# A delta-rule attention and gated feed-forward kernel: joins unit by unit, the second pair's joins moved into the first pair's hops, far corrections behind a copy

## The chip, the cores and the metric

One core of one Trainium2 chip runs the kernel. The metric is the device time of one execution in microseconds (us). A profile gives, for one execution, a span (from the first to the last recorded instruction) and the start and length of each instruction. TensorE is called PE (its weight loads PEld), VectorE DVE, ScalarE ACT, GpSimd POOL, SyncE SP.

## The reference

Two parts follow each other. The first is a delta-rule recurrence over time for 4 batches and 8 heads, with sequences of 768 and heads of 48:

```
k_n = k / (norm(k) + 1e-6)
for t in range(768):
    y[t]  = q[t] @ state
    v_old = k_n[t] @ state
    state = state + beta[t] * outer(k_n[t], v[t] - v_old)
```

The second takes y as x, 3072 tokens by 384, through a feed-forward layer with w_in (384 by 2048) and w_out (2048 by 384):

```
h = x @ w_in
out = (h * sigmoid(1.702 * h)) @ w_out
```

The weights w_in and w_out arrive as 64-bit floats; the kernel turns them into 32-bit ones itself.

## The kernel before

**Units.** The sequence is cut into 6 chunks of 128 steps; a unit is one chunk of one batch, 24 in all. Units 0 to 3 (chunk 0 of the four batches) are of class `Step` and are worked on as two pairs, units 0 and 1, then 2 and 3. All later ones are of class `Half` and go through `slot`; the change leaves those alone.

**The solve of one unit.** Within a chunk the recurrence is a triangular system. It is cut into four blocks of 32 steps (`NB`, `BS`). The inverse of each 32 by 32 diagonal block is computed on DVE in halves of 16 (`invert`), and `merge` joins the halves of the first chunk: a product psP of 32 small matmuls per unit, a copy by ACT, a product psZ of 32 small matmuls and one of 128 by 128 per unit, a copy back by ACT. `merge` also transposes the inverses on DVE. Then a unit goes block by block: `solve` multiplies a block's right-hand side by the block's inverse (one 32 by 32 matmul for each of 8 heads, into psU), `solved` copies the result to SBUF on ACT, `below` multiplies it into the blocks underneath (into psV, for every head and every block below), and `rest` copies the next block's sum out of psV on ACT. Two units alternate: a hop is one call of `together`, which solves a block of one unit and does the `below` of the other. A pair takes 8 hops. The program's matmuls in 32-bit floats appear as two instructions each in the profile: 8 solves are 16 instructions.

**What stands around the hops.** Every engine runs its instructions in the order in which the program gives them (most go through `pinned`, which keeps program order). `fill(us)` puts pieces of the weight conversion into the program: DVE operations, and one ACT operation for each piece, called the clamp here (the Relu in `conversion`, with `low` as bias), that DVE waits for one piece later. `feed` puts three feed-forward products (ph) of the first tokens into the program. `warm(n)` puts in matmuls whose result is not used. `turn` transposes the keys of a later unit (psT), `gram` multiplies them (psG), `send_blocks` and `load_diagonals` bring the diagonal blocks through DRAM to the lanes of DVE (NT). `roots_second` scales the keys of units 4 to 7. `paced` lets POOL hold back a transfer of w_in until a hop is done; `fetch_out` starts a transfer of w_out. `put_out` makes the outputs (psY) and state of a unit, and ACT and small DMAs bring them to xT, which the ph products read.

**Order before.** Both joins of units 0 and 1, mixed with the scores of unit 3 and warm matmuls; 8 hops of the first pair (psU, psV), with four `turn`, two `gram` and warm matmuls between them; two `put_out`; both joins of units 2 and 3; then 8 hops of the second pair with a `feed` behind each; two `put_out`; a loop of 25 steps with `fill(1.0)` and `feed` each, in which DVE inverts the diagonal blocks of units 4 to 7 (`invert(1)`) and ACT scales keys; then the out products (po) of the first tokens, which start with 16 of one kind, and `slot` for the rest of the run.

Of the kernel before, what the change touches and what calls it, by code (L numbers as in the profile page):

```python
# [18 lines left out]
def kernel(  # L19
# [23 lines left out]
    C = 128  # L43
# [337 lines left out]
    def fill(us):  # L381
        while us > 0:
            us -= next(behind, us)
# [82 lines left out]
    def roots_second(areas):  # L466

        z, r = (TW[:, a : a + B * H].rearrange("p (b h) -> p b h", b=B) for a in (1792, 1856))
        for o in range(2):
            vec.tensor_reduce(z[:, 2 * o : 2 * o + 2], areas[o], axis=AX.X, op=ALU.add)  # L470
        pool.tensor_tensor(r, z, half[:, 0:1].broadcast_to([128, B, H]), op=ALU.pow)
        yield
        vec.tensor_scalar(r, r, 1e-6, None, op0=ALU.add)
        vec.reciprocal(r, r)
        for o in range(B):
            K = home(B + o)[:, :, 0:D]
            vec.tensor_tensor(K, K, r[:, o].broadcast_to([128, H, D]), op=ALU.mult)
            if o % HB == 1:
                yield
# [254 lines left out]
    def merge(pair, area, banks):  # L734

        XT, Pm = (
            [area[:, a + i * n : a + (i + 1) * n].rearrange("p (h k) -> p h k", h=H) for i in range(HB)]
            for a, n in ((0, H * BS), (HB * H * BS, H * BS // 2))
        )
        Z, HS = [inverse[X.n] for X in pair], BS // 2  # L740
        rows = [slice(k * BS, (k + 1) * BS) for k in range(NB)]
        for X, t in zip(Z, XT):
            vec.transpose(t.rearrange("p h k -> p (h k)"), X.rearrange("p h k -> p (h k)"))
        for X, x, m in zip(pair, Z, Pm):
            ps = banks[0][0].tile([128, H, HS], F32, tag=banks[0][1], name="psP")
            for h in range(H):
                for r in rows:
                    pe.matmul(
                        ps[r, h, :], lhsT=X.G[r, h, r], rhs=x[r, h, HS:], start=True, stop=True,
                        skip_group_check=True,  # L750
                    )
            act.activation(m, ps, ACT.Copy, scale=upper)
            yield
        for x, t, m in zip(Z, XT, Pm):
            ps = banks[1][0].tile([128, H, HS], F32, tag=banks[1][1], name="psZ")
            pe.matmul(ps, lhsT=ident, rhs=x[:, :, HS:], start=True, stop=True, skip_group_check=True)
            for h in range(H):
                for r in rows:
                    pe.matmul(
                        ps[r, h, :], lhsT=t[r, h, :], rhs=m[r, h, :], start=False, stop=True,  # L760
                        skip_group_check=True,
                    )
            act.copy(x[:, :, HS:], ps)
            yield

    def bank(name, shape=(128, H, D), big=False):
        if late:
            return one_bank(name)[:, 0 : H * D].rearrange("p (h d) -> p h d", h=H)
        from_, tag = (ps_big, "big") if big else (ps_seq, "seq")
        return from_.tile(list(shape), F32, tag=tag, name=name)  # L770
# [3 lines left out]
    class Step:  # L774
# [63 lines left out]
        def gather(self):  # L838
# [3 lines left out]
                start=True, stop=True, skip_group_check=True,  # L842
            )

        def below(self, blk, h, psR):
            r = slice(blk * BS, (blk + 1) * BS)
            for k in range(blk + 1, NB):
                u = slice(k * BS, (k + 1) * BS)
                pe.matmul(
                    self.psV[u, h, :], lhsT=self.G[r, h, u], rhs=self.U[r, h, :],  # L850
                    start=False, stop=True, skip_group_check=True,
                )

        def rest(self, blk, psR):
            u = slice((blk + 1) * BS, (blk + 2) * BS)
            act.copy(self.V[u], self.psV[u])

        def solve(self, blk, h, psU):
            r = slice(blk * BS, (blk + 1) * BS)
# [429 lines left out]
    def together(solves, belows):  # L1289

        solves = [(X, blk) for X, blk in solves if X]
        belows = [(X, blk) for X, blk in belows if X]
        psU = bank("psU") if solves else None
        psRs = [bank("psR") if X.n >= B else None for X, blk in belows]
        for h in range(H):
            for X, blk in solves:
                X.solve(blk, h, psU)
            for (X, blk), psR in zip(belows, psRs):
                X.below(blk, h, psR)
        for X, blk in solves:  # L1300
            X.solved(blk, psU)
        for (X, blk), psR in zip(belows, psRs):
            X.rest(blk, psR)
# [139 lines left out]
    for X in pair[:2]:  # L1443
        X.gather()
    warm(NY // 2)
    scaling = roots_second(areas)
    next(scaling)

    def paced(sign, i, j):

# [18 lines left out]
    products = merge(pair[:2], area, ((ps_seq, "seq"), (ps_big, "big")))  # L1469
    path, later = hops(*pair[:2]), hops(*pair[2:])  # L1470
    scored = pair[-1].scored
    for _ in range(HB):
        next(products)
        next(scored)
        warm(NM // 2)
    next(products)
    paced(inverse[0][0:1, 0, BS // 2 : BS // 2 + 1], 2, 1)
    fill(3.0)
    next(scaling)
    warm(NM)  # L1480
    Nds = []
    for i in range(2 * NB):
        together(*next(path))
        if i in (0, 1, 3, 5):
            at = pair[i % 2].US[i // 2 * BS : i // 2 * BS + 1, 0:1]
            paced(at, *{0: (2, 2), 1: (3, 0), 3: (3, 1), 5: (3, 2)}[i])
        if i == 0:
            warm(NM // 2)
            run(products)
            run(scored)  # L1490
            run(scaling)
        if i == 1:
            for X in pair[:2]:
                X.select()
        if i == 3:
            for b in range(HB, B):
                load_values(b, sync)
        if 1 <= i <= B:
            turn(B + i - 1)
        if i in (5, 6):  # L1500
            gram(B + i - 5)
        if i < 2 * NB - 1:
            warm(NU if i == 1 else NU // 2)
        if i == 6:
            Nds.append(send_blocks(B))
        if i > 5:
            fetch_out(i - 6, other_queue)
        fill(2.1 if i else 1.0)
    put_out(pair[0])
    merging = merge(pair[2:], area, ((ps_big, "big"), (ps_big, "big")))  # L1510
    fill(2.0)
    put_out(pair[1])
    Nds.append(send_blocks(B + 1))
    fetch_out(2, other_queue)
    for X in pair[2:]:
        next(merging)
        X.gather()
        warm(NM // 4)
    fill(4.0)
    for at in range(B):  # L1520
        for u in range(2):
            for half_ in range(2):
# [19 lines left out]
    ffn.append(hidden(xTs[0], gTs[0], slice(0, NTH), 1.3))  # L1542
    for i in range(2 * NB):
        if i == 0:
            for _ in range(HB):
                next(merging)
                fill(1.0)
            feed()
        together(*next(later))
        if i < 2:  # L1550
            gram(B + HB + i)
        if i == 1:
            Nds.append(send_blocks(B + HB))
        if i == 2:
            load_diagonals(Nds + [send_blocks(B + HB + 1)])
        feed()
        fill(2.2)
# [102 lines left out]
```

## Time and profile before

| | |
|---|---|
| time, median of 3 runs | 690.48 us (686.99 to 691.98) |
| the profiled execution | 683.09 us, its span 681.4 us |
| PE busy | 660.4 us (97%), 9290 matmul instructions |
| DVE busy | 479.5 us (70%) |
| ACT busy | 233.6 us (34%) |
| POOL busy | 269.4 us (40%) |
| granted clock of PE | 0.991 of full speed over the span |
| first solve of the first pair | 45.47 us |
| first solve of the second pair | 78.66 us |
| first operation of `invert(1)` on DVE | 103.06 us |
| first po matmul | 143.25 us |

The busy shares are means over stages with different limits. The rows that matter here lie in the first 155 us: the hops of the two pairs, and the stretch in which DVE converts weights and inverts.

### The profile page before, as it was taken

Reading aid. Unit: us, or ns where it says so; the run is one execution under the profiler, and the core shown is the slowest. Engines: PE = TensorE matmul, PEld = TensorE weight load, DVE = VectorE, ACT = ScalarE, POOL = GpSimd, SP = SyncE. Lnnn points to the kernel's source line nnn. Section 1 sums busy time; section 2 is a strip of 40 time slices with the busy share of each in tenths; the row PEclk is TensorE's granted clock in tenths of the full one; section 3 lists DMA queues with packets and bytes.
Section 4 is the critical chain, followed back from the end, with each engine's and each line's share of the span. In section 5 each row is a group of like instructions: output and inputs, shape, how many; then the busy total and the mean of one; then the engine's idle time right before and its main releaser. Section 6 shows DMA issues by size and latency. Waiting matters only on the chain.

```text
span 681.4 us, 21731 instructions
## 1 busy us (share of the span) xinstructions
PE 660.4 (97%) x9290; PEld 563.4 (83%) x9290; DVE 479.5 (70%) x890; ACT 233.6 (34%) x571; POOL 269.4 (40%) x282
## 2 busy tenths in 40 slices
PE   9899899799999999999999999999999999999997
PEld 4766678566678998998998988988988988989997
DVE  4889799983788997996997996997976970200000
ACT  2558463632333233333333233233233233322120
POOL 4032844320286634635535526426305205105041
PEclk9799999989999999999999999999999999999999
DMA  9567575263334435335335244244231130100101
GB/s 174 105 165 175 128 218 99 44 155 81 83 74 92 96 63 109 79 67 104 71 67 116 67 90 88 66 86 79 62 78 19 38 75 2 30 2 6 26 0 24
DMA packets 149632, 54.61 MB, mean 80 GB/s; under 512 B 137824, under 2 KB 142656, under 8 KB 149536
## 3 DMA queue, kind: packets, MB, share of 16 engines
q1 hardware_dynamic: 146368, 46.62, 32.7%
q0 software_dynamic: 3168, 6.61, 3.7%
q8 instruction: 73, 1.20, 0.8%
q14 instruction: 23, 0.19, 0.1%
HBM read 38.37 MB, written 13.63 MB: 76 GB/s over the span
## 4 chain that ended last, share of the span: by engine, by line
PE 86%; DVE 6%; ACT 2%; DMA 2%; issue 2%; SPq 1%; DVEq 0%; ACTq 0%
PE po L139 34%; PE ph L139 32%; PE four L139 7%; PE psU L139 3%; PE psR L139 2%; PE psG L139 2%; DVE P L139 2%; DVE w_out L139 2%; PE ps_warm L139 1%; DVE YB L139 1%; DMA TW<-in_q_dram 1%; PE psQ L139 1%; SPq L139 1%; PE psV L139 1%; DVE NT L139 1%
## 5 line engine op out<-in xcount | busy, mean ns | idle before, releaser
L139 PE MATMUL ph<-xT,w_in 128*128 128x256 f32 x1152 | 261.0, 384 | 2.3 <-ACT gT L139 2.0
L139 PEld LDWEIGHTS ph<-xT,w_in 128*128 128x128 f32 x1152 | 215.9, 190 | 33.8 <-ACT gT L139 2.4
L1118 POOL TENSOR_TENSOR gT<-gT 128x512 f32<-128x512 f32 x80 | 103.0, 1298 | 97.9 <-ACT gT L139 66.0
L139 PE MATMUL po<-w_out,gT 128*128 128x192 f32 (+1 forms) x720 | 138.4, 347 | 0.0
L139 DVE TENSOR_TENSOR P<-NT,YB 64x8 f32<-64x8 f32 (+13 forms) x195 | 124.8, 640 | 5.8
L139 PEld LDWEIGHTS po<-w_out,gT 128*128 128x128 f32 x720 | 118.5, 190 | 11.0 <-ACT o L139 0.5
L139 ACT ACTIVATE gT<-ph 128x512 f32<-128x512 f32 x90 | 53.8, 598 | 154.8 <-PE ph L139 154.8
L139 DVE TENSOR_REDUCE YB<-P 64x4 f32<-64x8 f32 (+13 forms) x195 | 78.4, 402 | 6.7
L139 PE MATMUL po<-TW,gT 128*128 128x192 f32 x480 | 81.8, 328 | 0.0
L139 PEld LDWEIGHTS po<-TW,gT 128*128 128x128 f32 x480 | 78.1, 190 | 0.7
L984 POOL TENSOR_SCALAR_AFFINE_SELECT M<-M 64x512 f32<-64x512 f32 x40 | 29.1, 727 | 90.0 <-ACT M L139 88.8
L139 DVE TENSOR_TENSOR o<-o,late 128x192 f32<-128x192 f32 x20 | 6.6, 356 | 68.1 <-ACT late L139 67.9
L139 ACT COPY VU<-psU 32x384 f32<-32x384 f32 x96 | 45.2, 470 | 21.3 <-PE psU L139 14.9
L139 DVE TENSOR_TENSOR VU<-VU,psR 32x384 f32<-32x384 f32 x40 | 22.1, 553 | 36.6 <-PE psR L139 35.9
L400 POOL TENSOR_TENSOR rn<-ssq,half 128x8 f32<-128x8 f32 x12 | 22.3, 1858 | 52.6 <-DVE ssq L139 52.6
L139 DVE TENSOR_TENSOR VU<-VU,four 128x384 f32<-128x384 f32 x19 | 10.4, 548 | 46.1 <-ACT M L139 46.0
L109 POOL DMA_DIRECT2D KN<-in_k_dram x24 | 17.2, 716 | 58.4 <-PE four L139 56.7
L139 ACT COPY o<-po 128x192 f32<-128x192 f32 (+1 forms) x44 | 14.7, 334 | 74.6 <-PE po L139 72.5
L139 PEld LDWEIGHTS psU<-VU,XBs 32*32 32x32 f32 x1536 | 27.4, 105 | 13.5 <-issue 8.5
L139 PE MATMUL psU<-VU,XBs 32*32 32x48 f32 x1536 | 32.6, 203 | 0.3 <-ACT VU L139 0.2
L139 DVE TENSOR_TENSOR P<-NT 64x512 f32<-64x512 f32 (+7 forms) x45 | 30.5, 679 | 1.1
L139 DVE TENSOR_REDUCE NT<-P 64x32 f32<-64x512 f32 (+9 forms) x45 | 30.0, 668 | 1.5
(167 smaller groups left out, 752.1 us busy)
## 6 DMA issues: line engine op xcount, KB each, us to landing
VU<-in_v_dram SPq DMA_DIRECT2D x40, 96.0 KB, 2.8
out_dram<-o SPq DMA_DIRECT2D x40, 96.0 KB, 2.2
QW<-in_q_dram SPq DMA_DIRECT2D x76, 48.0 KB, 2.2
Kd<-KN SPq DMA_DIRECT2D x56, 64.0 KB, 2.2
late<-Kd SPq DMA_DIRECT2D x14, 256.0 KB, 2.8
KN<-in_k_dram POOLq DMA_DIRECT2D x30, 96.0 KB, 3.1
w_out<-in_moe_w_out_dram SPq DMA_DIRECT2D x7, 384.0 KB, 3.8
NT<-Nd SPq DMA_DIRECT2D x20, 128.0 KB, 2.7
```

Source lines behind the costliest of these rows:

```text
L109: dma(out=place(dst, n)[rows, :, 0:D], in_=src[b, :, t, :].rearrange("h p d -> p h d"),)
L139: return lambda *a, **kw: tc.keep_in_program_order(op(*a, **kw))
L400: nc.gpsimd.tensor_tensor(rn, ssq, half, op=ALU.pow)
L984: nc.gpsimd.affine_select(out=M, in_=M, compare_op=ALU.is_gt, fill=0.0, base=0, pattern=[[0, H], [1, CH]], channel_multiplier=-1,)
L1118: (engine or nc.gpsimd).tensor_tensor(o, a, b, op=op)
```

## The change

In `merge`, one unit's psP, copy, psZ and copy now come together before those of the next unit. In `below`, a unit of class `Step` multiplies only into the next block; the blocks further down get theirs in `rest`, after the copy of the next block, in one product that is 64 columns wide for the first block and 32 for the second. `together` does all solves of a hop and their copy, then all `below` and `rest`, where it took them head by head in turn. Around the hops: the first solve comes between the two joins of its pair; the joins of units 2 and 3 are called in hops 5, 6 and 7 of the first pair and after its `put_out`; `roots_second` starts behind the first join and its scalings come behind hops 2 and 3; the warm matmuls are fewer; `turn` of units 4 and 5 comes in hops 3 and 4, of unit 6 after the `put_out`, of unit 7 in hop 0 of the second pair; all four `gram` come in hops 1 to 4 of the second pair, their `send_blocks` in hops 2 to 4, `load_diagonals` after hop 5; three `fetch_out` come together after the `put_out` of the first pair; the amounts of `fill` up to the second pair's first hop go from 26.7 to 23.7; and the second pair's first hop has two `feed` ahead of it.

```
@@ merge
-        for X, x, m in zip(pair, Z, Pm):
+        for X, x, t, m in zip(pair, Z, XT, Pm):
             ps = ... name="psP"
...
             act.activation(m, ps, ACT.Copy, scale=upper)
             yield
-        for x, t, m in zip(Z, XT, Pm):
             ps = ... name="psZ"
@@ class Step
+        def add(self, blk, h, u):
+            r = slice(blk * BS, (blk + 1) * BS)
+            pe.matmul(
+                self.psV[u, h, :], lhsT=self.G[r, h, u], rhs=self.U[r, h, :],
+                start=False, stop=True, skip_group_check=True,
+            )
+
         def below(self, blk, h, psR):
-            r = slice(blk * BS, (blk + 1) * BS)
-            for k in range(blk + 1, NB):
-                u = slice(k * BS, (k + 1) * BS)
-                pe.matmul(
-                    self.psV[u, h, :], lhsT=self.G[r, h, u], rhs=self.U[r, h, :],
-                    start=False, stop=True, skip_group_check=True,
-                )
+            self.add(blk, h, slice((blk + 1) * BS, (blk + 2) * BS))
 
         def rest(self, blk, psR):
             u = slice((blk + 1) * BS, (blk + 2) * BS)
             act.copy(self.V[u], self.psV[u])
+            if blk + 2 < NB:
+                for h in range(H):
+                    self.add(blk, h, slice((blk + 2) * BS, C))
@@ together
+        if all(X.n < B for X, blk in solves + belows):
+            for X, blk in solves:
+                for h in range(H):
+                    X.solve(blk, h, psU)
+                X.solved(blk, psU)
+            for X, blk in belows:
+                for h in range(H):
+                    X.below(blk, h, None)
+                X.rest(blk, None)
+            return
@@ the first pair
-    scaling = roots_second(areas)
-    next(scaling)
...
-    for _ in range(HB):
-        next(products)
-        next(scored)
-        warm(NM // 2)
+    next(products)
+    next(scored)
+    scaling = roots_second(areas)
+    next(scaling)
+    next(products)
     next(products)
     paced(inverse[0][0:1, 0, BS // 2 : BS // 2 + 1], 2, 1)
-    fill(3.0)
-    next(scaling)
-    warm(NM)
+    fill(2.0)
     Nds = []
+    slots["xT"] = wk.tile([128, 2 * DM], I32, tag="xT", name="raw", bufs=3)
+    merging = merge(pair[2:], area, ((ps_big, "big"), (ps_big, "big")))
     for i in range(2 * NB):
         together(*next(path))
...
         if i == 0:
-            warm(NM // 2)
-            run(products)
+            next(products)
+            next(scored)
+        if i == 1:
             run(scored)
-            run(scaling)
-        if i == 1:
+            warm(NM // 4)
             for X in pair[:2]:
                 X.select()
+        if i == 2:
+            warm(NU // 2)
+            next(scaling)
         if i == 3:
+            run(scaling)
             for b in range(HB, B):
                 load_values(b, sync)
-        if 1 <= i <= B:
-            turn(B + i - 1)
-        if i in (5, 6):
-            gram(B + i - 5)
-        if i < 2 * NB - 1:
-            warm(NU if i == 1 else NU // 2)
-        if i == 6:
-            Nds.append(send_blocks(B))
-        if i > 5:
-            fetch_out(i - 6, other_queue)
-        fill(2.1 if i else 1.0)
+        if i in (3, 4):
+            turn(B + i - 3)
+            warm(NM // 2)
+        if i > 4:
+            next(merging)
+            warm(NM // 4)
+        fill(1.9)
     put_out(pair[0])
-    merging = merge(pair[2:], area, ((ps_big, "big"), (ps_big, "big")))
     fill(2.0)
     put_out(pair[1])
-    Nds.append(send_blocks(B + 1))
-    fetch_out(2, other_queue)
+    next(merging)
     for X in pair[2:]:
-        next(merging)
         X.gather()
         warm(NM // 4)
-    fill(4.0)
+    turn(B + HB)
+    fill(3.0)
+    for f in range(3):
+        fetch_out(f, other_queue)
@@ the second pair
         if i == 0:
-            for _ in range(HB):
-                next(merging)
-                fill(1.0)
-            feed()
+            feed(2)
+            fill(1.5)
         together(*next(later))
-        if i < 2:
-            gram(B + HB + i)
-        if i == 1:
-            Nds.append(send_blocks(B + HB))
-        if i == 2:
+        if i == 0:
+            turn(B + HB + 1)
+        if 1 <= i <= B:
+            gram(B + i - 1)
+        if 2 <= i <= B:
+            Nds.append(send_blocks(B + i - 2))
+        if i == B + 1:
             load_diagonals(Nds + [send_blocks(B + HB + 1)])
         feed()
         fill(2.2)
```

## The prediction

> **What bounds the kernel now.** I read first the busy time by stage (columns: window, length, then busy us of PE, PEld, DVE, ACT and POOL, the granted clock, DMA share and GB/s).
>
> ```profile
> core 0: us, PE busy (x) PEld busy (x) DVE busy (x) ACT busy (x) POOL busy (x), PEclk, DMA share, GB/s
> 38.70:64.10 25.40, 23.81 (x716) 16.49 (x714) 23.54 (x35) 16.48 (x36) 10.39 (x10) 1.00 0.67 155
> 64.10:77.20 13.10, 9.05 (x333) 6.97 (x331) 12.36 (x24) 6.01 (x17) 7.32 (x14) 1.00 0.52 116
> 77.20:98.60 21.40, 21.19 (x442) 16.54 (x440) 17.26 (x30) 13.94 (x29) 14.67 (x21) 1.00 0.77 219
> 98.60:136.80 38.20, 32.36 (x227) 27.21 (x226) 36.34 (x78) 18.94 (x61) 15.67 (x14) 1.00 0.38 79
> ```
>
> The rows are the first pair's joins and hops, its outputs with the second pair's joins, the second pair's hops, and the inversion. DVE is the full engine in the first, second and fourth; PE is full in the third (21.19 of 21.40), where DVE has 4.1 us free. In the fourth PE is idle 5.84 us. Behind it the chain that ended last is PE to the end, so what moves the first po product at 143.3 moves the end by as much. Next, pieces of that chain (start, length, engine, tile, instructions):
>
> ```profile
> 77.24 1.49 PE ph L139 x6
> 78.73 0.79 PE psU L139 x16
> 79.52 0.69 PE psG L139 x32
> ...
> 103.06 1.23 DVE NT L139
> ...
> 136.84 1.73 PE psQ L139 x32
> ...
> 153.83 0.80 PE psU L139 x32
> ```
>
> The way to po: the second pair's hops on PE, the conversion on DVE up to the inversion at 103.06 (NT), the keys scaled by ACT, psQ at 136.84. Note the two psU: 16 instructions take 0.79 us, 32 take 0.80. The 16 lie on one 32 by 32 patch of PE's array (one block, 8 heads), the 32 on two patches. The timeline shows how:
>
> ```profile
> 78.66 0.73 PEld L139 LDWEIGHTS psU<-VU,XBs 32*32 32x32 f32 x16 [0.33 <-issue]
> ...
> 84.51 0.24 PE L139 MATMUL psV<-VU,G 32*32 32x48 f32 x3
> 84.57 0.20 PE L139 MATMUL psU<-VU,XBs 32*32 32x48 f32 x1
> ```
>
> On one patch a load starts every (0.73 - 0.10)/15 = 0.042 us. In an interleaved hop the psV products run on other patches within 0.01 us of a psU, and the hop of 64 instructions from 84.50 ends at 85.38, 0.88 us, as long as 16 alone. Then who holds DVE:
>
> ```profile
> 79.56 0.47 ACT L139 COPY VU<-psU 32x384 f32<-32x384 f32 x1 [2.02 <-PE psU L139]
> 80.20 0.66 ACT L139 ACTIVATE G<-psG 128x256 f32<-128x256 f32 x2 [0.17 <-PE psG L139]
> 81.68 0.60 ACT L139 ACTIVATE gT<-ph 128x512 f32<-128x512 f32 x1 [0.82 <-PE ph L139]
> 82.17 0.61 ACT L139 ACTIVATE w_out<-w_out,low 128x384 int32<-128x384 int32 x1
> ```
>
> ```profile
> 45.48 0.18 DVE L139 TENSOR_SCALAR TW<-TW 128x32 f32<-128x32 f32 x1 [1.41 <-POOL TW L139]
> 82.81 1.03 DVE L139 SCALAR_TENSOR_TENSOR w_out<-raw,w_out 128x384 int32<-128x384 int32 x1 [3.45 <-ACT w_out L139]
> ```
>
> DVE waited 3.45 us for a clamp that stood behind gT on ACT, and gT behind ph on PE. ACT runs in order, so a slower PE hop becomes idle DVE.
>
> **The change, part by part.** The order of the built program agrees with the diff: 8 psU, 8 psV, then 8 wider psV that wait for ACT.
>
> *A hop.* Before, the least is 0.86 on PE, 0.04, two copies (0.47 + 0.49), 0.05: 1.9 us. After, solves and near products follow each other on one patch each, 16 x 0.042 = 0.67 apiece. Solve starts at 0; the copy of U runs 0.91 to 1.38; near ends its loads at 1.34, its last result 0.2 later; the copy of V runs 1.55 to 2.02; the far product stands behind that copy and starts at 2.07. Its own price has no row. At the least it is 0.67, as with 32 columns. The nearest row is this:
>
> ```profile
> 65.50 0.62 PE L139 MATMUL psY<-VU,KN 128*64 128x48 f32 x16
> ```
>
> 16 instructions of 64 columns, alternating between two halves, (0.62 - 0.22)/15 = 0.027 each, so 0.053 on one and 16 x 0.053 = 0.85. psG, also 64 columns, 32 instructions on four patches in 0.69, gives (0.69 - 0.2)/7 = 0.07, or 1.1, as the upper end. I take 0.9 for 64 columns, near psY's, and 0.67 for 32. Next to nothing overlaps, because PE takes matmuls in order: if solve, near and far could overlap as interleaved ones do, a hop would be back at about 2.1 (ends kept). So a hop lasts 2.97 (far 64; hops 1, 2), 2.74 (far 32; 3, 4) or 1.34 of PE with 2.07 to the next solve (5, 6).
>
> [...]
>
> *First pair.* Joins: psP 38.74; DVE's transposes now stand ahead of the 0.92 and 0.95 reductions, so psZ of unit 0 ends at 40.9 and psP of unit 1 at 41.6. The first copy of U waits behind a clamp (0.94) to 42.95, the other join's copy ends at 43.7, and two psQ stand ahead: hop 1 starts at 44.1 (before 49.08). Hop 1: 2.97, then psQ 0.71 and its two copies 0.65, which hold the next psU: hop 2 at 48.5. Hop 2: U waits for a clamp to 49.45, then 0.47, 0.49, far 0.9, warm 0.75: hop 3 at 52.1. Hop 3: 2.74, psT 0.6, warm 0.5: hop 4 at 55.95. Hop 4, with kT (0.60) and a clamp (0.94) ahead of U: 59.8. Hop 5, with psP 0.66 and warm, 2.25: 62.05. Hop 6, with psZ 1.0: 64.75. Hop 7 ends with psP: `put_out` at 66.3, 2.2 later than 64.10. Bounds -3 (overlap) and +2.
>
> *To the second pair.* `put_out` took 64.10 to 69.94, with one 1.49 us instruction stall: 66.3 to 72.1. The last xT transfer was issued 71.6, and took a median 2.6: 74.2; 2.2 later 76.4. The joins of 69.07 to 77.17 shrink to one psZ (1.0), psV 0.9 and psT 0.6, done by 74.8, so ph starts at 76.4, not 77.17. Two `feed` take 3.05: first solve 79.45 against 78.66 (0.8 late; bounds -3 and +2.5). POOL's three `fetch_out` now follow its xT transfers, about 74 to 76, and land 4 us later, against DVE's first use at 75.02 before; DVE is 3 us of fill less far on, and their clamp only runs in hop 1: no cost. The 16 bL transfers behind them (9.31 us) are first needed at NT.
>
> *Second pair.* Here PE had nothing idle, so all is paid. Hop 0: 0.67 + psT 0.5 + ph 1.5 = 2.67. Hops 1, 2: 2.97 + psG 0.62 + ph 1.5 = 5.09 each. Hops 3, 4: 4.86. Hops 5, 6: 1.34 + 1.5 = 2.84. Hop 7: 2.17. Sum 30.4, from 79.45 to 109.9; before it ended at 98.6. Of the difference, near is 4.0, far 3.1, waits for V 4 x 0.7 = 2.8, psG and psT moved here 1.8. One `feed` is done earlier.
>
> *DVE.* Its 1.41 us wait for POOL goes (the scaling now comes after POOL's 5.45 us op has ended), but clamps come with the longer hops: the one of hop 1 now ends at about 88, where DVE would stand at 78 by its work. With 3 us less fill the clamp of the last wide w_out piece stands in hop 7, behind ph (109.9): gT 0.6, clamp 0.93, 111.5. From the operation that uses it (98.5) to NT was 4.5 us: NT at 116.0, against 103.06, 12.95 late. NT's transfers are issued behind hop 5, at about 106 to 110, and land some 4 us later: in time, with little to spare.
>
> *Behind it.* NT to psQ was 33.78 us. In the new order the last rn pair comes two steps of the inversion earlier (0.61 + 0.62 + 0.64 + 0.69 = 2.56): psQ at 147.2. PE's own work from 98.6 to 136.8 was 32.36, less one feed of 1.5: it would be there at 140.8 and waits. From psQ to po was 6.48; now psQ 1.73, one ph 1.5 (2.39 at the lower clock that followed the 3.59 us idle here), psT 0.44, its copy, uncovered, 0.65, psG 0.62: 5.3. po starts at 152.5 against 143.3: **9.2 us later**. The inverse comes back through DRAM as before with 10 us in hand.
>
> So the profiled execution, 683.09 us around a span of 681.4, would take 692.3. It lies 7.4 below the median of the runs; on the median, 690.48 + 9.2 = **699.7**. Its own range is 694 to 706 (entry bounds, far price, a longer idle at psQ).
>
> **Rivals.**
> *No difference.* Solve, near and far overlap in part and the uncovered wait is short: hops 1 to 4 lose 4 x 0.8 and each near 0.3, 5 us less, and the entry is 3 earlier; 9.2 - 8 = 1.2, so 691.7. For it: three stages had DVE as bound. Against: 16 psU alone take as long as 64.
> *Faster.* The products hide in the copies' waits, and PE reaches the second pair early since 5.5 us of joins left the path. Then DVE loses its waits (1.41 + 3.45) and the 2.56 of order, but PE has only 5.84 idle to give: 690.48 - 5.8 = 684.7. It decides once a hop of the second pair, with ph, stays under about 3 us; before they were 2.4 to 3.1. Against: PE was full there.
> *The clock falls.* With fewer warm matmuls PE idles about a quarter of each first-pair hop. From 17 to 20 us PE was busy 1.51 of 3.00 and the clock then fell to 0.50. At half clock 19 products of 0.67 take 12.7 more: 690.48 + 9.2 + 12.7 = 712. Against: 64.10 to 77.20 was 69% busy at 1.00.
> [...]
>
> **How the numbers follow.** Forecast 0.62, no difference 0.16, faster 0.15, clock 0.07. About 1% (6.9 us) can be told from no change. Slower by more: 0.55 of the forecast's 0.62 and the clock, 0.62. Within: 0.07 + 0.16 = 0.23. Faster: 0.15. The range of 687 to 707 leaves out most of the faster case and the clock.
>
> **What would show it.** Right: psU and psV in separate runs of 0.7 us each, a psV that waits for ACT in hops 1 to 4; second-pair hops of about 5 us; DVE idle behind clamps, some 20 us between 64 and 116; NT near 116 and po near 152. Wrong: hops under 3 us, NT before 106, or po before 145.

## The result and the profile after

The changed kernel takes 719.06 us (median of 4 runs, 715.12 to 725.71) against 690.01 for the kernel before on the same chip: 4.4% longer, a ratio of 1.0435 with a 95% interval of 1.0332 to 1.0538. The forecast was 9.2 us more; it is 29. The profiled execution took 715.12 us around a span of 713.4. Two things are needed to read the numbers below: executions of before differ in their mean granted clock (its profiled one had 0.991 and took 683.09, most others about 0.977 and 691), and the comparisons leave out executions that lie over 1.5% above a kernel's fastest.

First the busy time by stage of the changed kernel, with the same columns as in the prediction: first pair's joins, its hops, `put_out` with what is left of the second pair's joins, the second pair's hops, then up to psQ.

```profile
core 0: us, PE busy (x) PEld busy (x) DVE busy (x) ACT busy (x) POOL busy (x), PEclk, DMA share, GB/s
38.74:43.66 4.92, 1.99 (x132) 1.77 (x132) 4.82 (x7) 0.99 (x3) 3.43 (x1) 0.88 0.61 128
43.66:84.92 41.26, 39.03 (x599) 31.92 (x590) 20.01 (x34) 14.50 (x30) 5.79 (x8) 0.50 0.37 75
84.92:96.54 11.62, 10.25 (x154) 8.01 (x153) 6.05 (x11) 3.93 (x12) 6.84 (x12) 0.91 0.39 118
96.54:132.30 35.76, 33.19 (x471) 26.84 (x470) 18.91 (x34) 15.73 (x34) 16.19 (x24) 0.86 0.56 140
132.30:171.04 38.74, 32.89 (x227) 27.35 (x227) 35.69 (x77) 20.09 (x62) 13.90 (x13) 1.00 0.34 71
```

The granted clock stands behind the counts. In the first pair's hops it is 0.50 for 41 us, although PE is busy for 39.03 of them; before, the clock was 1.00 in the four rows of the prediction. The second pair's hops have 0.86 on the mean: 1.00 at first, lower from 104 us on. PE is now the full engine of both pairs, and DVE, which was full in the first, is busy half of the time.

Next the timeline (start, length, engine, tile, instructions, and in brackets the wait ahead of it): the stall in the joins, hop 1 of the first pair, hop 1 of the second, and the three marks of the way to po.

```profile
42.88 0.98 PE L139 MATMUL psP<-XBs,gT 32*32 32x16 f32 x58 [2.93 <-issue]
...
48.36 1.24 PE L139 MATMUL psU<-VU,XBs 32*32 32x48 f32 x13
...
49.58 1.24 PE L139 MATMUL psV<-VU,gT 32*32 32x48 f32 x13
51.37 1.94 PE L139 MATMUL psV<-VU,gT 32*64 32x48 f32 x16 [0.56 <-ACT VU L139]
...
99.22 0.73 PE L139 MATMUL psU<-VU,XBs 32*32 32x48 f32 x13
...
99.91 0.71 PE L139 MATMUL psV<-VU,G 32*32 32x48 f32 x13
...
100.66 0.47 ACT L139 COPY VU<-psV 32x384 f32<-32x384 f32 x1
101.18 1.13 PE L139 MATMUL psV<-VU,G 32*64 32x48 f32 x16 [0.56 <-ACT VU L139]
102.23 0.69 PE L139 MATMUL psG<-kT 48*64 48x64 f32 x32
102.86 1.56 PE L139 MATMUL ph<-xT,w_in 128*128 128x256 f32 x6
104.35 0.73 PE L139 MATMUL psU<-VU,XBs 32*32 32x48 f32 x13
...
137.69 1.22 DVE L139 TENSOR_TENSOR NT<-NT,bL 128x1024 f32<-128x1024 f32 x1
...
171.04 1.00 PE L139 MATMUL psQ<-QS,kT 48*64 48x112 f32 x32 [1.16 <-ACT QS L139]
...
175.33 1.88 PE L139 MATMUL po<-w_out,gT 128*128 128x384 f32 x5
```

Both hops have the forecast's form: solves, near products, the copy of V on ACT, a wait, the wide far product. In the second pair the hop from 99.22 to 104.35 lasts 5.13 us, at full clock (forecast 5.09). In the first pair the same instructions take 1.24 for 0.73 and 1.94 for 1.13. po starts at 175.3 instead of 143.3: 32.0 later, and the span is 32.0 longer, so the loss lies ahead of po, as the prediction's chain had it.

Last, what DVE waited for from 36 to 180 us (total, number, longest):

```profile
DVE w_in L139 <- ACT w_in L139: 27.7, 8, 7.5
DVE w_out L139 <- ACT w_out L139: 16.1, 6, 6.7
```

These are the clamps, 43.8 us together. On ACT those of w_in stand mostly behind copies that wait for PE in the first pair, those of w_out behind gT, and gT behind ph. Between 64 and 116 us, for which some 20 were forecast, it is 24.7 (21.5 and 3.2).

### The profile page after: what moved, and what is told of

Read it like the earlier page. It is cut to its first block, busy times and chain, and to the rows that moved or that the text cites. A ratio compares the mean times of both kernels' runs of the same rounds, so it can differ in the third digit from the quotient of the medians.

```text
span 713.4 us, 21552 instructions
## 1 busy us (share of the span) xinstructions
PE 687.8 (96%) x9203; PEld 590.1 (83%) x9203; DVE 476.8 (67%) x890; ACT 233.3 (33%) x571; POOL 267.7 (38%) x282
## 3 DMA queue, kind: packets, MB, share of 16 engines
q8 instruction: 72, 1.18, 0.7%
## 4 chain that ended last, share of the span: by engine, by line
PE 87%; DVE 6%; ACT 2%; issue 2%; DMA 1%; POOL 1%; DVEq 0%; ACTq 0%; POOLq 0%
PE po L139 32%; PE ph L139 32%; PE four L139 7%; PE psU L139 4%; PE psV L139 2%; PE ps_warm L139 2%; DVE P L139 2%; PE psR L139 2%; DVE YB L139 2%; PE psG L139 1%; DMA bL<-in_beta_dram 1%; DVE NT L139 1%; ACT VU L139 1%; PE psT L139 1%; PE psZ L139 1%
## 5 line engine op out<-in xcount | busy, mean ns | idle before, releaser
L139 PE MATMUL ph<-xT,w_in 128*128 128x256 f32 x1152 | 264.0, 387 | 5.0 <-ACT TW L139 3.6
L139 PEld LDWEIGHTS psU<-VU,XBs 32*32 32x32 f32 x1536 | 32.0, 110 | 14.3 <-issue 10.7
L139 PE MATMUL psU<-VU,XBs 32*32 32x48 f32 x1536 | 37.3, 209 | 0.0
```

The source lines that it names most:

```text
L139: return lambda *a, **kw: tc.keep_in_program_order(op(*a, **kw))
```

## The experiments

Theory A: the clock fell because warm matmuls were taken out. Theory B: the new hop works on one patch (32 by 32) of PE's array at a time, and the clock goes by how much of the array works, not by how long PE is busy. Theory C: the stall of 2.93 us, marked "issue" and read here as a wait for instructions, started it. (No view shows what PE waited for; the page of the changed kernel has a DMA queue of the kind "instruction", 72 packets and 1.18 MB in all.) The factor behind each time is that of its own comparison, with its 95% interval.

### The parts of the change

**warm_back.** The changed kernel with before's warm matmuls.

```
+    warm(NM // 2)   # twice between the joins' steps; warm(NM) ahead of the hops
...
+        if i < 2 * NB - 1:
+            warm(NU if i == 1 else NU // 2)
```

> The changed kernel with the warm matmuls of before again in the joins and behind each hop of the first pair; all else as changed. Theory A (the warm matmuls taken out let the granted clock fall at 40 us and keep it at 0.50 to 84 us): the clock stays at 1.00 from 40 to 84, put_out starts near 67 instead of 84.9, and the time falls from 719 to about 700, which is the forecast without the clock (699.7). Theory B (one 32 by 32 patch at a time does not count as work for the clock, whatever stands between): the clock still falls to about 0.5 in the hops, and with more warm matmuls at half speed the time is 716 or more.

724.79 us, 1.0471 (1.043 to 1.0511): no gain. From 40 to 96 us:

```profile
40.00:96.00 56.00, 51.74 (x743) 38.14 (x736) 23.65 (x38) 15.05 (x32) 9.21 (x8) 0.50 0.30 65
```

The clock was 0.50 with PE busy 51.74 of 56 us. Theory A falls in its simple form: three warm matmuls behind a hop are not enough.

**hops_back, hop_only, serial_below, near_inter.** The hop alone, and its two parts: the serial order (all solves, then the products below) and the far product behind the copy of V.

```
hops_back     changed kernel, `below`, `rest` and `together` of before
hop_only      kernel before, `add`, `below`, `rest` and `together` of the changed one
serial_below  changed kernel, in `below`:
-            self.add(blk, h, slice((blk + 1) * BS, (blk + 2) * BS))
+            for k in range(blk + 1, NB):
+                self.add(blk, h, slice(k * BS, (k + 1) * BS))
              and no far product in `rest`
near_inter    changed kernel, without the branch in `together`
```

> The changed kernel with the hops of before (solve and below head by head in turn, all blocks below in one go); the new schedule and its few warm matmuls stay. Theory A (missing warm matmuls): the clock falls at about 40 us as in the changed kernel, since the joins are the same, and stays low through the first pair; the time is about 705 to 712, the hops being shorter at either clock. Theory B (the serial order on one patch): the clock, once fallen in the joins, is back at 1.00 within a few hops, the second pair starts near 77, and the time is 690 or less.

> The kernel of before with the new hop alone (all solves, their copy, the near products, the copy, the wide far product); joins, schedule and warm matmuls of before. Theory A: the clock stays at 1.00 over 36 to 100 us and the hop alone costs what the prediction's sum gave it: in the second pair 4.0 (near) + 3.1 (far) + 2.8 (waits) = 9.9 us, of which the wait at psQ takes little, so about 699 (ratio 1.013). Theory B: the clock falls in the first pair's hops as it did in the changed kernel, and the time is 708 or more.

> The changed kernel with one part of the hop undone: the products into all blocks below come ahead of the copy of V again, one 32 by 32 product for each; still all solves first, then the copy of U, then these. Theory B (one patch at a time lowers the clock): the products into three or two blocks alternate between patches of the same rows and other columns, the solves stay on one patch; if the solves are enough to hold the clock down it stays at 0.5 through the first pair and the time is 706 or more; if not, it comes back in the hops and the time is about 694. A rival, that the far product (its width and its wait for V) holds the clock down: the clock comes back within two hops, and the time is 694 or less.

> The changed kernel with the other part of the hop undone: solve and near product alternate head by head as before, and only the far product stays behind the copy of V. Theory B: two patches work at a time in most of the hop, so the clock comes back before the second pair, and the time is 690 to 702: no near run (4.0 us less in the second pair's hops), the far products still cost 3.1 and their waits 2.8. The rival (the far product holds the clock down): the clock stays at 0.5 until the xT wait, and the time is 708 or more.

| | products of all blocks ahead of the copy | far product behind the copy of V |
|---|---|---|
| head by head | hops_back 690.27, 1.0008 (0.9983 to 1.0033) | near_inter 714.76, 1.0345 (1.0284 to 1.0406) |
| serial | serial_below 696.56, 1.0068 (1.0044 to 1.0092) | the changed kernel 719.06, 1.0435 (1.0332 to 1.0538) |

The far product, with the wait ahead of it, costs 714.76 - 690.27 = 24.5 us with the one order and 22.5 with the other. The serial order costs 6.3 and 4.3; the second lies within the intervals of its two kernels. The rest of the change, new schedule and joins, costs nothing: 1.0008. And the hop put into the kernel of before takes 729.57, 1.0558 (1.0528 to 1.0589), 39 us more, four times the 9.9 us that the prediction's prices give for it. Why it costs more there than in the new schedule (29) was not taken apart.

My expectation for near_inter was wrong. I had taken the serial solves for the cause, and two patches at a time for enough. That for serial_below was wrong too: its clock stayed at 0.50 up to 80 us, for which I had expected 706 or more. The second pair's hops tell why not; first serial_below, then near_inter, same columns:

```profile
84.00:114.00 30.00, 28.37 (x525) 22.45 (x516) 23.65 (x41) 16.73 (x36) 22.53 (x36) 1.00 0.70 184
```

```profile
96.00:100.00 4.00, 2.96 (x83) 2.48 (x82) 3.90 (x9) 1.31 (x4) 2.24 (x5) 1.00 0.31 99
100.00:128.00 28.00, 24.93 (x334) 19.06 (x334) 9.78 (x20) 10.42 (x24) 11.84 (x18) 0.63 0.59 142
```

With the far product and its wait the clock falls again a hop after it was at 1.00; without them it stays up. In near_inter it is, from the first solve of the second pair to that of its last hop, 93.55 to 129.51, 36.0 us, against 91.21 to 113.38, 22.2, in serial_below. Of these 13.8 us the prediction's prices at full clock (3.1 for the far products, 2.8 for the waits) explain 5.9.

In hops_back theory A had the clock right and theory B the time:

```profile
44.00:72.00 28.00, 28.00 (x622) 21.41 (x622) 20.06 (x34) 13.83 (x29) 5.34 (x8) 0.50 0.52 111
76.00:104.00 28.00, 27.22 (x532) 20.95 (x532) 22.56 (x41) 17.53 (x38) 22.79 (x36) 1.00 0.75 194
```

The clock was at 0.50 through the first pair there too, but an interleaved hop at half clock is short enough that the second pair starts at 81.48, 2.8 later than before and 15.1 earlier than in the changed kernel.

### What the clock goes by

**clock_alone, clock_two.** Phases of matmuls on PE alone, each after 40 or more warm ones.

```
one:  240 x  t[0:32, h] from G[0:32, h, 0:32], X[0:32, h]
four: 110 x  the same for rows 0:32, 32:64, 64:96 and 96:128 in turn
...
for i in range(16): one(8); warm(1)     # then with warm(3), with warm(6)
```

> A kernel that computes nothing of the reference (its output is zeros): phases of f32 matmuls on PE, each after 40 warm matmuls of the whole array. One 32 by 32 patch (240 matmuls), four patches in turn (440), one patch 64 columns wide (100); then, each behind a pause of about 5 us, the whole array (24), four patches (520), one patch (240); then 8 rounds like a hop with one warm matmul each. Theory B: in the one-patch phases the granted clock falls to 0.5 though PE is never idle and stays there, and behind a pause it does not come back; with four patches in turn or the whole array it holds at 1.00 and comes back. Theory A: after the warm matmuls one patch holds 1.00 as well as four do, and behind a pause each phase is at 0.5 for a few us and then back at 1.00, whatever its patches.

> A second kernel that computes nothing of the reference (its output is zeros): phases after 40 warm matmuls each. Two patches of other rows and columns in turn (400 matmuls); one patch with 384 columns of data through each load (60); one patch, 8 matmuls, then 1, 3 or 6 warm matmuls, repeated; two patches of the same rows (400). If the clock goes by how much of the array works at a time: two patches give a clock between those of one (0.50) and four (1.00), 384 columns on one patch stay at 0.50, and 3 warm matmuls (0.64 us) to 0.67 us of one patch hold 1.00, being half of the time on the whole array. If it goes by weight loads instead (a load-bound PE looks idle to the clock): 384 columns on one patch hold 1.00, and two patches of any kind fall to 0.50.

Windows of clock_alone: one patch twice, four patches, 64 columns wide, the whole array, one patch again. (A pause was meant to stand ahead of the last two; the trace shows none on PE.)

```profile
24.00:28.00 4.00, 4.00 (x53) 4.00 (x52) 0.00 (x0) 0.00 (x0) 0.00 (x0) 0.50 0.02 4
40.00:44.00 4.00, 4.00 (x53) 4.00 (x52) 0.00 (x0) 0.00 (x0) 0.00 (x0) 0.50 0.00 0
76.00:80.00 4.00, 1.83 (x174) 1.70 (x163) 0.00 (x0) 0.00 (x0) 0.00 (x0) 1.00 0.02 4
100.00:104.00 4.00, 4.00 (x41) 4.00 (x40) 0.00 (x0) 0.00 (x0) 0.00 (x0) 0.50 0.00 0
120.00:124.00 4.00, 4.00 (x20) 3.51 (x20) 0.00 (x0) 0.00 (x0) 0.00 (x0) 1.00 0.00 0
196.00:200.00 4.00, 4.00 (x53) 4.00 (x52) 0.00 (x0) 0.00 (x0) 0.00 (x0) 0.50 0.00 0
```

On one patch PE is busy 4.00 of 4.00 us, and the clock is 0.50. On four patches in turn it is busy 1.83, stands still for the rest, marked "issue", 1.80 to 2.17 us at a time, and has 1.00. Busy time in the profile is not what the clock went by; in this respect theory B is right for one patch.

The same windows of clock_two (a program without ACT work, so that column is absent): two patches of other rows and columns, 384 columns of data through one patch, 8 products on a patch and 1 warm matmul, the same with 3, two patches of the same rows.

```profile
32.00:36.00 4.00, 4.00 (x106) 4.00 (x104) 0.00 (x0) 0.00 (x0) 0.50 0.01 4
80.00:84.00 4.00, 4.00 (x8) 1.15 (x7) 0.00 (x0) 0.00 (x0) 0.50 0.00 0
152.00:156.00 4.00, 4.00 (x39) 2.89 (x37) 0.00 (x0) 0.00 (x0) 0.50 0.02 4
184.00:188.00 4.00, 4.00 (x53) 2.38 (x51) 0.00 (x0) 0.00 (x0) 1.00 0.02 4
248.00:252.00 4.00, 4.00 (x108) 4.00 (x104) 0.00 (x0) 0.00 (x0) 0.50 0.00 0
```

Two patches are no better than one, 0.50 both times (I had expected a clock in between), and streaming through one load does not help, 0.50 with PEld busy 1.15 of 4.00 us, so it is not the weight loads. Nor is it the mean work of the array. First clock_two, then clock_alone, at full clock:

```profile
20.59 2.91 PE L19 MATMUL psTwo<-X,G 32*32 32x48 f32 x128 [0.18 <-issue]
24.04 19.93 PE L19 MATMUL psTwo<-X,G 32*32 32x48 f32 x513 [0.55 <-issue]
```

```profile
64.93 1.56 PE L19 MATMUL psFour<-X,G 32*32 32x48 f32 x128 [1.80 <-issue]
68.38 1.56 PE L19 MATMUL psFour<-X,G 32*32 32x48 f32 x128 [1.90 <-issue]
```

Two patches and four both got 128 equal matmuls in 3.45 us; the clock of the two then fell, to 0.63 from 24 to 28 us and 0.50 from there, that of the four stayed at 1.00 to 84 us, the end of their phase. How many patches work at the same time seems to count, and theory B holds in this form alone.

With one warm matmul for 8 products the whole array has 0.31 of 1.11 us at full clock, 28%: the clock falls. With three it has 0.75 of 1.55, 48%: it holds. The second pair's hops fit when only ph and warm matmuls are counted as whole-array work: ph is 1.49 of 5.13 us in the changed kernel (29%) and of 5.09 in near_inter (29%), and both fall; 1.49 of 3.46 in serial_below (43%) and of 2.93 in hops_back (51%), and both hold. Counted so, the limit for holding lies here between 29% and 43%, and the far product matters because it stretches the hop. What to count is a choice: with psG (0.63 us, four patches in turn) 41 and 42% fall, and the least that held is the 48% above. The limit is a fit, then, and no run moves the share in the hops alone.

These are hops without a stall. In the trace of hops_hot, whose hops are those of before, PE stood still for 1.16 us, marked "issue", inside a hop of the second pair (90.84 to 92.00), and the clock was 0.74, 0.50 and 0.91 in the three windows of 4 us from 92 on.

**clock_held, hop_held.** Only warm matmuls are added, in the wait for V and behind the hops of the first pair.

```
             act.copy(self.V[u], self.psV[u])
             if blk + 2 < NB:
+                warm(8)          # 4 matmuls
                 for h in range(H):
...
+        warm(NU)                 # 6 behind each hop; hop_held: in place of 3
```

> The changed kernel with work added and nothing taken away: 4 warm matmuls in each hop while PE waits for the copy of V, and 6 behind each hop of the first pair. If the clock is the whole of what was not forecast: with about half of PE's time on the whole array (in the second kernel without a reference 48% held 1.00 and some 25% did not) the clock is at 1.00 in the hops of both pairs, and though some 80 matmuls are added the time falls from 719 to between 700 and 712: the forecast 699.7, and at most 8 x 1.3 for the warm matmuls behind the hops and 8 x 0.2 for those in the waits. If something else holds the changed kernel back, the time rises to 725 or more.

> The kernel of before with the new hop, as in hop_only (729.6), and 4 warm matmuls in each wait for V and 6 behind each hop of the first pair, where it had 3. If the clock is what cost hop_only 39 us: clock 1.00 in the hops, and 699 (the hop alone as the prediction had it) to 708 (with 7 x 0.65 and 8 x 0.4 for the added matmuls). If the clock stays low: 735 or more.

hop_held took 708.96, 1.0248 (1.0207 to 1.0289): with 50 matmuls more than hop_only (32 in the waits, 18 behind the hops) it is 20.6 us faster, and 1 us outside the expectation. One window of each, hop_only over most of the second pair's hops and hop_held over the same:

```profile
108.00:140.00 32.00, 29.61 (x288) 24.06 (x288) 12.06 (x22) 10.49 (x22) 12.81 (x19) 0.61 0.50 136
```

```profile
96.00:124.00 28.00, 28.00 (x380) 21.46 (x373) 15.77 (x27) 12.77 (x27) 14.73 (x22) 1.00 0.59 166
```

More work on PE made the kernel faster, and with the clock at 1.00: this pair shows that some 20 of the 39 us, at least, are the clock's. In the 17 us that hop_held still loses are the hop's own price, the added matmuls and 12 us at half clock (44 to 56); they were not taken apart. clock_held took 716.44, 1.0328 (1.0242 to 1.0414), between the two ranges that I had given, and not clear of the changed kernel's 1.0435. Its clock is at 1.00 from about 61 us on, so what I had missed is the cost of holding it: up to 60 us the added matmuls still run at half clock, and a first-pair hop at full clock with 10 of them lasts 5.4 us (66.97 to 72.38), not much under the 6.3 that the same hop has at half clock without them (61.21 to 67.54). Its second pair is the forecast's hop at an undisturbed clock:

```profile
101.88 0.73 PE L139 MATMUL psU<-VU,XBs 32*32 32x48 f32 x13
102.57 0.71 PE L139 MATMUL psV<-VU,G 32*32 32x48 f32 x13
103.21 1.04 PE L139 MATMUL ps_warm<-ident 128*128 128x512 bf16 x4
104.18 1.13 PE L139 MATMUL psV<-VU,G 32*64 32x48 f32 x16
105.23 0.69 PE L139 MATMUL psG<-kT 48*64 48x64 f32 x32
105.86 1.56 PE L139 MATMUL ph<-xT,w_in 128*128 128x256 f32 x6
107.35 0.74 PE L139 MATMUL psU<-VU,XBs 32*32 32x48 f32 x13
```

The hop lasts 5.47: the far product starts 2.30 behind the solve instead of 2.07, since the warm matmuls outlast the wait, and takes 1.05 to the next start instead of 0.9; 5.09 + 0.23 + 0.15 = 5.47. Whole-array work without psG is 1.49 + 0.86 of it, 43%, and the clock holds. From the first solve to that of the last hop it took 29.70 (99.20 to 128.90) against 28.25 forecast.

**hops_warm, hops_hot.** hops_back with 3 and with 6 warm matmuls behind a hop, both with those of warm_back in the joins and without the changed kernel's few.

```
+            warm(NU if i == 1 else NU // 2)     # hops_warm
+            warm(NU)                            # hops_hot
```

> The changed kernel with the hops of before and also the warm matmuls of before in the joins and behind the hops of the first pair; only the new schedule stays. hops_back, without these warm matmuls, took 690.3 with a clock of 0.50 from 44 to 73 us. If warm matmuls count once the hops are interleaved, the clock is back at 1.00 within some 10 us of the joins, the second pair's entry comes some 5 us earlier and the time is about 685, under both kernels. If they count for nothing, they are only 20 more matmuls at half speed (about 0.4 us each on the path): 693 to 698.

> The new schedule with the hops of before and 6 warm matmuls behind each hop of the first pair (hops_warm had 3 and 698.7, hops_back 1 on the average and 690.3). A hop of four patches at a time and 6 warm matmuls is nearly all of the array's time at work, so the clock should be at 1.00 by about 55 us; at full speed the matmuls hide behind DVE, which sets the pace of these hops. Then the second pair starts at about 74 and the time is 683 to 688, under both kernels. If the clock does not come back so: 700 to 706.

hops_warm took 698.65, 1.0105 (1.0051 to 1.0159), with 0.50 from 44 to 84 us; hops_hot 688.56, 0.9953 (0.9916 to 0.999), with the clock back by 60 us; each lies about half a us outside its expectation. Coming back took more than holding: in hops_warm a hop of 2.83 us (58.60 to 61.43) had 1.39 of warm matmuls, 49%, and stayed at half clock.

### What starts the fall, and what is left to gain

**flood.** 640 matmuls on four patches, twice. The 9.4 MB of transfers were to run beside the second time; they started with the kernel and ran beside the first, which serves as well.

```
+    for f in range(8): nc.sync.dma_start(out=land[f], in_=src)   # 1.18 MB each
```

> A third kernel that computes nothing of the reference (its output is zeros): 640 matmuls on four patches in turn, once alone and once beside 9.4 MB of transfers that share the DMA engines. In clock_alone PE ran 128 of these instructions in 1.56 us and then waited 1.8 to 2.3 us for instructions, with the clock at 1.00. Theory C (the transfers delay the instruction fetch, and a wait of some 2.7 us is what lets the clock fall): beside the transfers the waits are 2.7 us or longer and the clock falls below 1.00. The rival (the wait for instructions is the same with and without transfers, and its length decides nothing): 1.8 to 2.3 us and 1.00 in both phases.

```profile
27.62 2.78 PE L19 MATMUL psFour<-X,G 32*32 32x48 f32 x128 [4.63 <-issue]
33.54 2.78 PE L19 MATMUL psFour<-X,G 32*32 32x48 f32 x128 [3.14 <-issue]
...
50.65 1.56 PE L19 MATMUL psFour<-X,G 32*32 32x48 f32 x128 [1.90 <-issue]
```

PE runs 128 of these matmuls with their 128 loads and then waits, marked "issue": 1.90 us alone from 50 us on, 2.09, 4.63 and 3.14 beside transfers at a DMA share of 1.00 to 1.09, and the clock is 0.50 from 24 to 36 us. That is the form of the stall of 2.93 us in the joins, where the share was 1.05 in the 4 us ahead of it and 0.60 in it. But the second time, at a share of 0.07 and less and with waits of 1.90 us at most up to the fall, the clock also fell for some 10 us (0.54, 0.50 and 0.68 from 84 to 96), so the long waits stood at one fall and not at the other.

The stall is not the change's own. Kernels with the schedule of before have it too, at the same place, and there too the clock is at 0.50 from 44 us on: 2.16 us in before_hot, 2.72 in hop_only, 2.67 in joins_only. In the profiled execution of before it was 1.00, and the clock stayed at 1.00. That fits theory C as a trigger; as no run takes the wait away alone, it is not shown. As the cause of a clock that stays low it falls: clock_alone falls with no wait at all.

**before_hot, joins_only, joins_hot.** The kernel before with 6 warm matmuls behind each hop; with the joins unit by unit alone; with both.

```
joins_only: `merge` of the changed kernel
before_hot: -            warm(NU if i == 1 else NU // 2)
            +            warm(NU)
            -        warm(NM // 4)      # behind each gather of the second pair
            +        warm(NM // 2)
joins_hot:  both
```

> The kernel of before with the joins unit by unit alone (psP, copy, psZ, copy of one unit, then the other), its schedule, hops and warm matmuls unchanged. If the order of the joins brings the clock down and the hops of before can't bring it back: clock 0.50 from 44 to some 75 us, 697 or more. If it takes the new schedule (first solve ahead of the other join, fewer whole-array matmuls between the first hops): clock at 1.00, and 688 to 692, no difference.

> The kernel of before with 6 warm matmuls behind each hop of the first pair (it had 3) and 4 about the second pair's joins (it had 2); nothing else. Most executions of before have a mean clock near 0.977 and take about 691, its profiled one had 0.991 and took 683: some 8 us seem to be lost to the clock in most of them. If warm matmuls bring it back sooner: 683 to 688. If not, or if they cost as much as they return: 690 to 694.

> The same with the joins unit by unit (joins_only took 689.1, with runs from 680.0). If the joins are worth their 2.6 us beside the clock and the warm matmuls bring it back sooner: 681 to 686, under both kernels; if the one takes the place of the other, as before_hot.

before_hot took 689.88, 1.0003 (0.9966 to 1.0041); joins_only 689.1, 0.9913 (0.9876 to 0.9949), with executions from 680.0 to 694.7; joins_hot 691.74, 1.0044 (1.0008 to 1.0079). By the medians of all executions, 689.1 against 691.66, joins_only is only 0.4% under. The joins alone do no harm, though in the profiled execution of joins_only the clock fell, and was back at 60 us. As joins_only and joins_hot lie on either side of no change, and hops_hot under by 0.5%, I do not claim a version that beats the kernel before by what can be told. That before itself loses some 8 us to the clock in most executions is argued from its mean clocks alone (0.977 against 0.991 or 0.987); before_hot and joins_hot, which were to remove it, gained nothing.

## Why the prediction was wrong

Its sign, its chain and its hop were right; the term for the clock was not.

*The hop.* Solve and near in separate runs of 0.7: so. The wait for V: 0.56 to 0.72. The far product 1.05 for 0.9, inside its bounds (0.67 and 1.1). A hop of 5.13 for 5.09. In clock_held, at full clock, a whole pair took 29.70 against 28.25, with the added matmuls for the difference. The rival "no difference", that solve, near and far overlap, is refuted: the far product waits for ACT, and solves and near products follow each other but for the last three. So is "faster": in the second pair no new hop that carries a far product came under 4.5 us.

*The clock.* The step that failed is the clock term: the forecast put it at nothing and gave the rival 0.07 and 12.7 us. The runs showed about 20 us in its place (14.4 in the first pair, 5.3 in the second) and part of 4.3 in the joins. Three things were wrong. First, the rival's reason was that PE would idle a quarter of each hop, but PE was busy 39.03 of the 41.26 us at 0.50. Second, no gap is needed. A low clock does stand behind long ones: in before PE idled 3.59 us ahead of psQ at 136.84 and had 0.51 from there to 140 us, and in the changed kernel 0.50 follows the stall of 2.93 us, with PE busy 1.12 of 4 us around it. But in clock_alone the clock went to 0.50 with PE busy 4.00 of 4.00 us: one small patch at work there, or two in clock_two, did not keep it up. The trace of before had shown as much:

```profile
17.00:20.00 3.00, 1.51 (x105) 1.19 (x99) 1.77 (x4) 1.52 (x3) 0.00 (x0) 1.00 0.06 7
20.00:23.00 3.00, 2.82 (x112) 2.65 (x88) 2.30 (x5) 0.28 (x1) 0.17 (x1) 0.65 0.02 5
23.00:26.00 3.00, 3.00 (x32) 3.00 (x32) 2.55 (x12) 2.17 (x4) 0.00 (x0) 0.50 0.62 114
```

The prediction cites the first of these rows. The longest gap on PE there is 1.49 us (ahead of the psD at 19.79, among matmuls of 32 columns), and the clock fell to 0.50. Third, the price went by 19 small products, but at half clock the rest of PE's work took longer too, up to twice its time and more (psQ 1.22 to 1.67 for 0.71, a warm matmul of clock_alone 0.43 for 0.215 from start to start), and the clock fell again in the second pair.

*The way to po,* by the prediction's own marks:

| | forecast | measured | difference added |
|---|---|---|---|
| first pair's hop 1 | 44.1 | 48.36 | +4.3 (stall, joins at half clock) |
| `put_out` | 66.3 | 84.92 | +14.4 (clock 0.50) |
| second pair's first solve | 79.45 | 96.54 | -1.5 |
| end of its hops | 109.9 | 132.3 | +5.3 (clock 0.79 from 104 to 128) |
| NT | 116.0 | 137.69 | -0.7 |
| po | 152.5 | 175.33 | +1.1 |

The sum is 22.8 us; with the 9.2 forecast it makes the 32.0 of the span. No row without the clock or the stall is off by more than 1.5, the last by luck in part: psQ came 33.35 behind NT where 31.2 was forecast, 2.15 late, and po 4.29 behind psQ where it was 5.3.

*What else was read wrongly.* The prediction treated before's clock of 1.00 as safe ("64.10 to 77.20 was 69% busy at 1.00"). It was probably the clock of a fortunate execution: joins_only and before_hot, with the hops of before, show 0.50 from 44 to nearly 60 us. That four patches at a time and 3 warm matmuls a hop held the clock there, both of which the change took away, is argued: hops_warm has both, and its clock, once fallen, stayed at 0.50 for 40 us.

## What to carry to other kernels

When a change takes matmuls on several patches apart into runs on one, price it twice: by its instructions at full clock, and by whether the whole array still has enough of the time (here 29% was too little and 43% enough, with psG left out of the count) for the clock to hold. A high busy share of PE in the profile said nothing on that (39.03 of 41.26 us at 0.50); the granted clock in windows of a few microseconds did. Warm matmuls have a price of their own: 32 in the waits and 18 behind the hops gained 20.6 us in hop_held, 32 and 48 cost nearly what they returned in clock_held.

## What the runs showed of the hardware

- One or two patches of the array, busy with waits of 0.55 us at most, had the clock at 0.50 within 3 to 8 us of the last warm matmul and to the end of the phase, some 11 to 69 us in clock_alone and clock_two. Four in turn, busy 1.56 to 2.12 of 4 us, had 1.00 in clock_alone from 64 to 84 and from 140 to 164 us; in the 8 us after that it was 0.83 and 0.75, behind a wait of 2.44 us. In flood it fell to 0.50 twice.
- To bring the clock back seems to take more whole-array work than to hold it: 49% of a hop did not in hops_warm, while 48% held it in clock_two and 43%, without psG, in clock_held. With six warm matmuls a hop it was back within some 14 to 17 us in hops_hot, before_hot and joins_hot, with 40 in a row within 2.7 to 5.4 in clock_alone and clock_two; but in joins_only, with the warm matmuls of before, it was back by 61 us too.
- In clock_alone and flood, with four patches in turn, PE ran 128 matmuls and 128 loads and then waited, marked "issue", at best one such lot in 3.45 us. In clock_alone the wait was 1.80 to 2.44 us of each 3.45 to 4.00, in flood up to 4.63 beside transfers. That it is a wait for instructions is the reading given with theory C.
